# Attention, a dense block and routed experts on one core: where the first expert's hidden rows leave PSUM, when the small group's rows are scaled, and a rank computation cut in two

## The chip, the cores and the metric

The kernel runs on one core of a Trainium2 chip. The time is device microseconds (us) of one execution; a kernel's time is the median of its runs. The kernel before was run three times: 752.45 us median, 751.44 to 753.85.

## What is computed

Three blocks in a row, in float32. Attention over 4 batches, 12 heads, 448 positions and 64 channels with a tanh cap on the scores; a dense block with a SoLU and a layer norm on the 1792 tokens that come out; and a mixture of 8 experts, in which every token goes to one expert:

```python
logits = x @ w_gate + modality_bias[modality_id]
e_idx = np.argmax(logits, axis=1)
...
for e in range(E):
    mask = e_idx == e
    h = np.maximum(x[mask] @ w1[e], 0.0)
    out[mask] = gate_w[mask, None] * (h @ w2[e])
```

Which tokens go to which expert is known only when the dense block has produced the logits of the last token tile.

## The kernel before

The 1792 tokens are 14 tiles of 128. Each float32 operand of a large product is split into a high part and a remainder (names ending in `h` and `l`; ScalarE, ACT, casts the high part, VectorE, DVE, subtracts it), and TensorE (PE) makes three products of them: high by high, high by low, low by high. Products collect in PSUM; ACT and DVE empty it.

The program runs in four stretches. Up to some 430 us, attention and most of the dense block are interleaved on PE. Then come the last token tiles of the dense block with the **routing** between them. Then the **first expert**, the one that most of the first ten tiles chose, with 256 tokens, which starts before the routing is complete. Then the **slots** of a fixed list, `D` (512 tokens), `H` (128), `D`, `F` (256), `H`, with two **small groups** `T` of 32 tokens served beside the two `D` slots. In these last stretches the order on every engine is the order in which the code is written: PE and DVE are held to it in the routing stretch, and all engines from the end of the first expert's first layer on.

The names that matter for the change:

- **Routing** (`route_group`, a generator that the driver steps with `next`). It runs for tiles 0 to 9, then for 10 to 12 (`ra`), then for 13 (`rb`). Its first stage (L256 to L266) makes one-hot rows `r_oh` of each token's expert from the logits `lg` (L654, read from the PSUM tile `y`) and their running count `cum`; the second (L273 to L306) makes each token's rank among its expert's tokens and from it the matrices `r_A` and `r_B`; the third multiplies these on PE into the list of tokens `r_pt` (L316). For tile 13 the counts of all experts follow (`route_counts`, L366 to L379), `route_sums` on PE, `r_cmp` (L395), and at the end the index tables by which GpSimd (POOL) gathers the slots' rows.
- **First expert.** `e_weights` loads a block of its weights into `e_raw` (three buffers, L1031, queue of SyncE, SP), and splits it on ACT (L1033) and DVE (L1034) into `winh`/`winl` (first layer) and `wouh`/`woul` (second). The driver interleaves these steps with the rest (`next(ew)`). `e_h` makes the first layer (L1048 to L1052): 6 blocks of depth `d` by 8 blocks `f` of 128 hidden channels by 3 products of 256 columns. It collects in two PSUM tiles `e_ph` of two banks each, blocks 0 to 3 in the first and 4 to 7 in the second. In the last depth block, after every second `f`, ACT writes `e_hh` (L1055) and DVE `e_hl` (L1056) from the two blocks that are complete. `e_o` makes the second layer (L1068 to L1070): 8 blocks `f` by two token tiles (`e_po`, two more PSUM tiles) by 6 products. PSUM tiles of this size come from a ring of three, so the second `e_po` lies where the first `e_ph` was.
- **Between the blocks of `e_o`** stands the preparation of the first slot (`lead`, `first`, in `run_slots`): before blocks 3 to 6 the transposes of D's four token tiles (`s_tr`, L1221 to L1225), each emptied by ACT and DVE and followed by a weight split `wh_D`, `wl_D` (L1190, L1191); before block 7 the small group: DVE scales its 32 gathered rows `ygT` (`t_sc`, L1340 to L1342) and PE transposes them (`t_tr`, L1349) into `tpT`. After `e_o` PE goes on with D's first layer (`s_h`, L1247 to L1249, PSUM `phD`).

Of the kernel before, what the change touches and what calls it, by code (L numbers as in the profile page):

```python
# [14 lines left out]
AF = mybir.ActivationFunctionType  # L15
ALU = mybir.AluOpType
# [9 lines left out]
ND = DM // P  # L26
# [60 lines left out]
def attn_moe_kernel(ctx, tc, qt, kt, vv, cap, w_in, w_out, g_ln, ids, w_gate, mbias, w1, w2, out):  # L87
# [164 lines left out]
    def route_group(K, tp, psR, atile, a, b):  # L252
        n = b - a
        oh = K["oh"][:, a:b, :]
        kk = tp.tile([P, n, NE], F32, name=f"kk{a}")
        dve.tensor_tensor(kk, lg[:, a:b, :], nmx[:, a:b].unsqueeze(2).to_broadcast([P, n, NE]), op=ALU.add)  # L256
        dve.scalar_tensor_tensor(kk, kk, 0.0, K["rev"][:, a:b, :], op0=ALU.is_equal, op1=ALU.mult)
        fm = tp.tile([P, n], F32, name=f"fm{a}")
        dve.tensor_reduce(fm, kk, axis=AX.X, op=ALU.max)
        dve.tensor_tensor(oh, kk, fm.unsqueeze(2).to_broadcast([P, n, NE]), op=ALU.is_equal)  # L260
        pr = atile(f"pr{a}")[:, 0, :n * NE].rearrange("p (t e) -> p t e", e=NE)
        prev = rstate.get("cum")
        last = b == NTILE
        cum = tp.tile([P, NE], F16, name=f"cum{a}")
        if n == 1:
            dve.tensor_tensor(cum, prev, oh[:, 0, :], op=ALU.add)  # L266
        yield
        mm = []
        if prev is not None:
            mm.append((pr, K["ones"], prev.unsqueeze(1).to_broadcast([P, n, NE])))  # L270
        for t in range(n - 1):
            mm.append((pr[:, t + 1:, :], K["ones"], oh[:, t:t + 1, :].to_broadcast([P, n - 1 - t, NE])))
        pe.matmul(pr, K["tri"], oh, start=True, stop=not mm)  # L273
        for i, (o, l, r) in enumerate(mm):
            pe.matmul(o, l, r, start=False, stop=(i == len(mm) - 1))
        if n > 1:
            cs = tp.tile([P, NE], F32, name=f"cs{a}")
            dve.tensor_reduce(cs, oh.rearrange("p t e -> p e t"), axis=AX.X, op=ALU.add)
            if prev is None:
                dve.tensor_copy(cum, cs)  # L280
            else:
                dve.tensor_tensor(cum, cs, prev, op=ALU.add)
        rstate["cum"] = cum
        if last:
            route_total(K)
        pm = tp.tile([P, n, NE], F32, name=f"pm{a}")
        dve.tensor_tensor(pm, pr, oh, op=ALU.mult)
        if last:
            yield
            r1 = route_counts(K, tp)  # L290
            yield
            route_sums(K, r1)
        rf = tp.tile([P, n], F32, name=f"rf{a}")
        dve.tensor_reduce(rf, pm, axis=AX.X, op=ALU.add)
        ri, pl, ph = (tp.tile([P, n], I32, name=f"{x}{a}") for x in ("ri", "pl", "ph"))
        dve.tensor_copy(ri, rf)
        dve.tensor_scalar(pl, ri, P - 1, None, op0=ALU.bitwise_and)
        dve.tensor_scalar(ph, ri, 7, None, op0=ALU.logical_shift_right)
        A, Bm = K["A"][:, a:b, :], K["B"][:, a:b]
        dve.tensor_tensor(A, K["io128"].unsqueeze(1).to_broadcast([P, n, P]),  # L300
                          pl.unsqueeze(2).to_broadcast([P, n, P]), op=ALU.is_equal)
        rm = tp.tile([P, n, NR], F16, name=f"rm{a}")
        dve.tensor_tensor(rm, K["io14"].unsqueeze(1).to_broadcast([P, n, NR]),
                          ph.unsqueeze(2).to_broadcast([P, n, NR]), op=ALU.is_equal)
        dve.tensor_tensor(rm, rm, K["tid"][:, a:b].unsqueeze(2).to_broadcast([P, n, NR]), op=ALU.mult)
        dve.tensor_tensor(Bm, oh.unsqueeze(3).to_broadcast([P, n, NE, NR]),  # L306
                          rm.unsqueeze(2).to_broadcast([P, n, NE, NR]), op=ALU.mult)
        if last:
            cmp_ = route_expert(K, tp)
        yield  # L310
        if last:
            pe.matmul(rstate["sm"][:1, 16:16 + NS], K["ones"][:NE, 0:1], cmp_.rearrange("p a b -> p (a b)"), start=True, stop=True)
        if a == 0:
            rstate["pt"] = psR.tile([NE * NR, P], F32, name="r_pt")
        for t in range(a, b):
            pe.matmul(rstate["pt"], K["B"][:, t].rearrange("p a b -> p (a b)"), K["A"][:, t, :],  # L316
                      start=(t == 0), stop=(t == b - 1), skip_group_check=True)
        if a == 0:
            route_early(K, tp, psR)
        if last:  # L320
            yield from route_end(K, tp)
# [673 lines left out]
    ee = {}  # L995
# [41 lines left out]
    def e_h():  # L1037
        xh, xl = ee["xh"], ee["xl"]
        ph = []
        hh, hl = ([mp.tile([P, 4, SLOT], F32R, tag="m4", name=f"e_{x}{q}", bufs=4) for q in range(2)] for x in ("hh", "hl"))  # L1040
        ee["hh"], ee["hl"] = hh, hl
        for d in range(ND):
            for f in range(NF):
                if d == 0 and f % 4 == 0:
                    ph.append(atile(f"e_ph{f // 4}").rearrange("p a (b c) -> p (a b) c", c=SLOT))
                o = ph[f // 4][:, f % 4, :]
                c = slice(f * P, (f + 1) * P)
                pe.matmul(o, winh[d][:, c], xh[:, d, :], start=(d == 0 and f % 2 == 0), stop=False, skip_group_check=True)  # L1048
                yield
                pe.matmul(o, winh[d][:, c], xl[:, d, :], start=False, stop=False, skip_group_check=True)  # L1050
                yield
                pe.matmul(o, winl[d][:, c], xh[:, d, :], start=False, stop=(d == ND - 1), skip_group_check=True)  # L1052
                if d == ND - 1 and f % 2:
                    q, r = f // 4, slice(f % 4 - 1, f % 4 + 1)
                    act.activation(hh[q][:, r, :], ph[q][:, r, :], AF.Relu)  # L1055
                    dve.scalar_tensor_tensor(hl[q][:, r, :], ph[q][:, r, :], 0.0, hh[q][:, r, :], op0=ALU.max, op1=ALU.subtract)  # L1056
                yield
    def e_o(step):
        po = [atile(f"e_po{i}") for i in range(2)]
        for f in range(NF):  # L1060
            step(f)
            for i in range(2):
                o = slice(i * P, (i + 1) * P)
                hh, hl = ee["hh"][f // 4][:, f % 4, o], ee["hl"][f // 4][:, f % 4, o]
                for hf in range(2):
                    c = slice(hf * HD, (hf + 1) * HD)
                    p = po[i][:, hf, :HD]
                    pe.matmul(p, hh, wouh[f][:, c], start=(f == 0), stop=False)  # L1068
                    pe.matmul(p, hh, woul[f][:, c], start=False, stop=False)
                    pe.matmul(p, hl, wouh[f][:, c], start=False, stop=(f == NF - 1))  # L1070
        for i in range(2):
            ob = g2.tile([P, DM], F32, tag="tm", name=f"e_ob{i}", bufs=NTM)
            act.activation(ob[:, :HD], po[i][:, 0, :HD], AF.Copy, scale=ga0[:, i:i + 1])
            dve.tensor_scalar(ob[:, HD:], po[i][:, 1, :HD], ga0[:, i:i + 1], None, op0=ALU.mult)
            pool.indirect_dma_start(out=oview("E", i), out_offset=IndirectOffsetOnAxis(ap=sidx0[:, i:i + 1], axis=0),
                                    in_=ob, in_offset=None, bounds_check=NT, oob_is_err=False)
# [18 lines left out]
    def run(k):  # L1095
        for _ in range(k):
            msteps.pop(0)[1]()
# [9 lines left out]
    with tc.manual_schedule(engines={ET.PE, ET.DVE}):  # L1107
        run(4)
        ra, rb = (route_group(K, rt, psR, atile, *x) for x in groups)
        ew = weights()  # L1110
        next(ra)
        next(ew)
        run(5)
        next(ra)
        run(3)
        next(rb)
        next(ew)
        run(3)
        next(ra, None)
        run(3)  # L1120
        next(rb)
        next(rb)
        next(ew)
        run(4)
        eh = e_h()
        for steps, subs in EHS:
            run_h(steps)
            next(rb, None)
            for _ in range(subs):
                next(ew)  # L1130
    hand = ExitStack()
    hand.enter_context(tc.manual_schedule())
    for _ in eh:
        pass
    for _ in ew:
        pass
    for pl_ in (rt, xp, wi, psR):
# [253 lines left out]
    def run_slots(seq, small, lead=None):  # L1391
# [48 lines left out]
        def first(i):  # L1440
            if i < len(cols(seq[0])):
                s_tr(seq[0], (i,))
            elif smalls:
                t_sc(smalls[0])
                t_tr(smalls[0])
                if smalls[1:]:
                    t_gather(smalls[1])
# [160 lines left out]
```

## Time and profile before

| | |
|---|---|
| median of 3 runs | 752.45 us (751.44 to 753.85) |
| the profiled execution's own time | 751.36 us |
| its span, first to last instruction | 749.6 us |
| PE busy | 724.3 us, 97% of the span |
| DVE, ACT, POOL busy | 59%, 52%, 16% |
| mean granted clock of PE | 0.994 of full speed |
| idle of PE from 430 us to the end, longest parts | 2.8, 1.6, 1.1 and 0.5 us |

Times are read from the start of the span. A timeline row is: start, duration, engine, line, operation, output and inputs, shapes, how many, and in brackets the idle time of the engine before it with what ended that. PE's matmuls overlap: the duration of one is longer than the step from one to the next, and what a stretch costs is counted in steps. PEld is PE's weight load, SPq the queue from which SP issues transfers.

### The profile page before, as it was taken

Reading aid. Unit: us, or ns where it says so; the run is one execution under the profiler, and the core shown is the slowest. Engines: PE = TensorE matmul, PEld = TensorE weight load, DVE = VectorE, ACT = ScalarE, POOL = GpSimd, SP = SyncE. Lnnn points to the kernel's source line nnn. Section 1 sums busy time; section 2 is a strip of 40 time slices with the busy share of each in tenths; the row PEclk is TensorE's granted clock in tenths of the full one; section 3 lists DMA queues with packets and bytes.
Section 4 is the critical chain, followed back from the end, with each engine's and each line's share of the span. In section 5 each row is a group of like instructions: output and inputs, shape, how many; then the busy total and the mean of one; then the engine's idle time right before and its main releaser. Section 6 shows DMA issues by size and latency. Waiting matters only on the chain. (4 is left out here: it accounts for less than half of the span.)

```text
span 749.6 us, 11324 instructions
## 1 busy us (share of the span) xinstructions
PE 724.3 (97%) x4302; PEld 557.8 (74%) x4302; DVE 438.6 (59%) x782; ACT 387.1 (52%) x535; POOL 116.7 (16%) x214
## 2 busy tenths in 40 slices
PE   6999999999999999999999999989999999999994
PEld 2443556667767777677788999988879998799983
DVE  7999656747666567555367447746156173663621
ACT  5999756774575654666521224244154162643530
POOL 4221101111031021120031211303010220002010
PEclk9999999999999999999999999999999999999998
DMA  9776211211121110110003103559918369484520
GB/s 300 250 237 198 62 53 47 63 60 51 45 83 38 58 59 13 60 34 13 21 23 127 44 22 106 184 207 318 406 57 275 113 204 407 180 276 170 201 96 23
DMA packets 33426, 97.14 MB, mean 130 GB/s; under 512 B 4903, under 2 KB 11057, under 8 KB 33362
## 3 DMA queue, kind: packets, MB, share of 16 engines
q1 hardware_dynamic: 26546, 66.88, 26.4%
q0 software_dynamic: 6528, 29.42, 11.0%
q8 instruction: 35, 0.57, 0.3%
q14 instruction: 29, 0.24, 0.1%
q10 hardware_dynamic: 288, 0.03, 0.0%
HBM read 85.24 MB, written 11.27 MB: 129 GB/s over the span
## 5 line engine op out<-in xcount | busy, mean ns | idle before, releaser
L735 ACT ACTIVATE e<-sc,sc 112x896 f32<-112x896 f32 x96 | 94.5, 1005 | 66.7 <-PE sc L728 66.7
L740 ACT ACTIVATE e<-e,cap_t 112x896 f32<-112x896 f32 x96 | 98.1, 1045 | 1.7
L770 PE MATMUL av<-e,v 112*64 112x448 f32 x384 | 82.8, 552 | 0.0
L650 PE MATMUL y<-wouh,lh 128*128 128x392 f32 (+1 forms) x224 | 77.9, 348 | 0.5 <-DVE lg L654 0.5
L652 PE MATMUL y<-wouh,ll 128*128 128x392 f32 (+1 forms) x224 | 75.8, 338 | 0.1
L651 PE MATMUL y<-woul,lh 128*128 128x392 f32 (+1 forms) x224 | 75.9, 339 | 0.0
L595 PE MATMUL h<-winh,xh 128*128 128x512 f32 x168 | 68.9, 410 | 0.0
L597 PE MATMUL h<-winh,xl 128*128 128x512 f32 x168 | 66.0, 393 | 1.1 <-DVE xl L583 1.1
L596 PE MATMUL h<-winl,xh 128*128 128x512 f32 x168 | 65.6, 390 | 0.0
L770 PEld LDWEIGHTS av<-e,v 112*64 112x64 f32 x384 | 23.3, 136 | 35.4 <-issue 33.4
L650 PEld LDWEIGHTS y<-wouh,lh 128*128 128x128 f32 x224 | 42.0, 188 | 9.1 <-issue 7.1
L1191 DVE TENSOR_TENSOR wl_D<-raw_D,wh_D 128x768 fp32r<-128x768 f32 (+1 forms) x28 | 29.8, 1071 | 26.9 <-ACT wh_D L1190 26.6
L1191 DVE TENSOR_TENSOR wl_H<-raw_H,wh_H 128x768 fp32r<-128x768 f32 (+1 forms) x28 | 29.2, 1069 | 25.6 <-ACT wh_H L1190 25.6
L595 PEld LDWEIGHTS h<-winh,xh 128*128 128x128 f32 x168 | 31.6, 188 | 16.4 <-issue 9.3
L1320 PE MATMUL poD<-wh_D,hhD 128*128 128x384 f32 x128 | 43.0, 336 | 0.0
L1321 PE MATMUL poD<-wl_D,hhD 128*128 128x384 f32 x128 | 42.8, 334 | 0.0
L1322 PE MATMUL poD<-wh_D,hlD 128*128 128x384 f32 x128 | 42.8, 334 | 0.0
L652 PEld LDWEIGHTS y<-wouh,ll 128*128 128x128 f32 x224 | 42.1, 188 | 0.8 <-DVE ll L640 0.8
L651 PEld LDWEIGHTS y<-woul,lh 128*128 128x128 f32 x224 | 42.1, 188 | 0.6
L1190 ACT CAST wh_D<-raw_D 128x768 fp32r<-128x768 f32 (+1 forms) x28 | 26.1, 932 | 27.3 <-DMA raw_D<-in_w_dram 27.0
L1190 ACT CAST wh_H<-raw_H 128x768 fp32r<-128x768 f32 (+1 forms) x28 | 25.3, 941 | 25.5 <-PE phD L1248 7.6
L597 PEld LDWEIGHTS h<-winh,xl 128*128 128x128 f32 x168 | 31.5, 188 | 8.8 <-DVE xl L583 2.0
(373 smaller groups left out, 1605.8 us busy)
## 6 DMA issues: line engine op xcount, KB each, us to landing
rawc<-in_w_out_dram POOLq DMA_DIRECT2D x16, 384.0 KB, 4.3
rawc<-in_w_in_dram POOLq DMA_DIRECT2D x12, 512.0 KB, 4.3
raw_D<-in_w_dram SPq DMA_DIRECT2D x12, 512.0 KB, 5.7
wr_T<-in_w_dram SPq DMA_DIRECT2D x16, 384.0 KB, 6.9
raw_D<-in_w_dram SPq DMA_DIRECT2D x16, 384.0 KB, 4.3
wr_T<-in_w_dram SPq DMA_DIRECT2D x12, 512.0 KB, 9.8
raw_H<-in_w_dram SPq DMA_DIRECT2D x12, 512.0 KB, 6.6
raw_H<-in_w_dram SPq DMA_DIRECT2D x16, 384.0 KB, 3.7
```

The source lines that it names most:

```text
L595: pe.matmul(o, s["xh"][d], winh[d][:, c], start=(d == 0), stop=False)
L596: pe.matmul(o, s["xh"][d], winl[d][:, c], start=False, stop=False)
L597: pe.matmul(o, s["xl"][d], winh[d][:, c], start=False, stop=(d == ND - 1))
L650: pe.matmul(o, s["lh"][f], wouh[f][:, c], start=(f == 0), stop=False)
L651: pe.matmul(o, s["lh"][f], woul[f][:, c], start=False, stop=False)
L652: pe.matmul(o, s["ll"][f], wouh[f][:, c], start=False, stop=(f == NF - 1))
L735: act.activation(e, t[:CK, :, :S], AF.Tanh, scale=sc8[:CK])
L740: act.activation(e, e, AF.Exp, scale=cap_t[:CK])
L770: pe.matmul(o[64 * j:64 * j + 64, :S], v[:, c, 64 * j:64 * j + 64], et[b, p, c][:, j, :], start=(c == 0), stop=(c == 3))
L1190: act.copy(h_, raw)
L1191: dve.tensor_sub(l_, raw, h_)
L1320: pe.matmul(p, hh[:, f, o], wh[:, c], start=(f == 0), stop=False)
```

## The change

Three edits.

1. In `e_h` the emptying of the first `e_ph` tile stands after block 3, for the whole tile; that of the second stands after the end of `e_h`, behind two more weight steps. Each is done as before in two halves of 512 columns, ACT and then DVE.
2. The scaling of the small group's rows stands behind the first of D's four transposes, in place of just before its own.
3. In `route_group` a stop is added after `pm` for all but the last tile, so that for tiles 10 to 12 the second stage comes in two pieces, and the driver puts the first stage of tile 13 between them, makes the `r_pt` products three steps later, and one weight split (`winl_132`, depth block 3) after tile 13's counts.

```diff
@@ route_group
             r1 = route_counts(K, tp)
             yield
             route_sums(K, r1)
+        else:
+            yield
@@ e_h
-                if d == ND - 1 and f % 2:
-                    q, r = f // 4, slice(f % 4 - 1, f % 4 + 1)
-                    act.activation(hh[q][:, r, :], ph[q][:, r, :], AF.Relu)
-                    dve.scalar_tensor_tensor(hl[q][:, r, :], ph[q][:, r, :], 0.0, hh[q][:, r, :], op0=ALU.max, op1=ALU.subtract)
+                if d == ND - 1 and f == 3:
+                    e_relu(ph, 0)
                 yield
+        ee["ph"] = ph
+
+    def e_relu(ph, q):
+        hh, hl = ee["hh"][q], ee["hl"][q]
+        for i in range(2):
+            r = slice(2 * i, 2 * i + 2)
+            act.activation(hh[:, r, :], ph[q][:, r, :], AF.Relu)
+            dve.scalar_tensor_tensor(hl[:, r, :], ph[q][:, r, :], 0.0, hh[:, r, :], op0=ALU.max, op1=ALU.subtract)
@@ the driver
         run(3)
         next(rb)
-        next(ew)
-        run(3)
+        next(ra)
+        run(6)
         next(ra, None)
-        run(3)
         next(rb)
         next(rb)
+        next(ew)
         next(ew)
         run(4)
@@
     for _ in eh:
         pass
+    next(ew)
+    next(ew)
+    e_relu(ee["ph"], 1)
     for _ in ew:
         pass
@@ first, in run_slots
             if i < len(cols(seq[0])):
                 s_tr(seq[0], (i,))
+                if i == 0 and smalls:
+                    t_sc(smalls[0])
             elif smalls:
-                t_sc(smalls[0])
                 t_tr(smalls[0])
```

How the order of instructions moves, at three places. The number behind a name is that of the buffer; the changed kernel's line numbers are 2 to 12 higher.

**DVE in the routing stretch, before.** `r_B` is the last step of the second stage for tiles 10 to 12, `lg` to `cum_4272` belong to tile 13, `e_xl` is the low part of the first expert's rows.

```order
L306 TENSOR_TENSOR r_B<-r_oh,rm_4250 128x336
L654 SCALAR_TENSOR_TENSOR lg<-y_4216,sm_4106,bias_t 128x8
L656 TENSOR_REDUCE nmx<-lg 128x1
L256 TENSOR_TENSOR kk_4265<-lg,nmx 128x8
L257 SCALAR_TENSOR_TENSOR kk_4265<-kk_4265,r_rev 128x8
L259 TENSOR_REDUCE fm_4268<-kk_4265 128x1
L260 TENSOR_TENSOR r_oh<-kk_4265,fm_4268 128x8
L266 TENSOR_TENSOR cum_4272<-cum_4211,r_oh 128x8
L1034 TENSOR_TENSOR winl_132<-e_raw_3_4274,winh_126 128x1024
L1016 TENSOR_TENSOR e_xl<-e_xt_4280,e_xh 128x6x128
```

The same engine in the changed kernel, from the piece `pm` of tiles 10 to 12 on:

```order
L287 TENSOR_TENSOR pm_4239<-pr_4210,r_oh 128x24
L656 SCALAR_TENSOR_TENSOR lg<-y_4216,sm_4106,bias_t 128x8
L658 TENSOR_REDUCE nmx<-lg 128x1
L256 TENSOR_TENSOR kk_4252<-lg,nmx 128x8
L257 SCALAR_TENSOR_TENSOR kk_4252<-kk_4252,r_rev 128x8
L259 TENSOR_REDUCE fm_4255<-kk_4252 128x1
L260 TENSOR_TENSOR r_oh<-kk_4252,fm_4255 128x8
L266 TENSOR_TENSOR cum_4259<-cum_4211,r_oh 128x8
L296 TENSOR_REDUCE rf_4261<-pm_4239 128x3
```

and further on, behind tile 13's counts, of which the last two rows stand here:

```order
L380 TENSOR_SCALAR r_wn<-r_dv 8x1
L381 COPY r_wn<-r_wn 8x1
L1036 TENSOR_TENSOR winl_132<-e_raw_3_4334,winh_126 128x1024
L1036 TENSOR_TENSOR winl_133<-e_raw_4_4338,winh_127 128x1024
L296 TENSOR_REDUCE rf_4374<-pm_4318 128x1
```

Tile 13's seven steps, from `lg` to `cum`, moved ahead of the eight from `rf` to `r_B`; `winl_132` moved from ahead of `e_xl` to behind the counts `r_wn`, and stands ahead of the rank of tile 13 (`rf_4374`), at whose end `r_cmp` is.

**ACT at the end of the first expert's first layer, before** (the queue behind the cast of block 3 of `wouh`):

```order
L1033 CAST wouh_138<-e_raw_3_4471 128x768
L1055 ACTIVATE e_hh_4356<-e_ph_4360 128x512 x2
L1055 ACTIVATE e_hh_4357<-e_ph_4397 128x512 x2
L1033 CAST wouh_139<-e_raw_4_4588 128x768
L1033 CAST wouh_140<-e_raw_5_4592 128x768
L1033 CAST wouh_141<-e_raw_6_4596 128x768
L1033 CAST wouh_142<-e_raw_7_4600 128x768
```

and in the changed kernel:

```order
L1035 CAST wouh_138<-e_raw_3_4471 128x768
L1064 ACTIVATE e_hh_4356<-e_ph_4360 128x512 x2
L1035 CAST wouh_139<-e_raw_4_4584 128x768
L1035 CAST wouh_140<-e_raw_5_4588 128x768
L1064 ACTIVATE e_hh_4357<-e_ph_4397 128x512 x2
L1035 CAST wouh_141<-e_raw_6_4596 128x768
L1035 CAST wouh_142<-e_raw_7_4600 128x768
```

Two casts, whose rows wait for transfers, moved between the two PSUM tiles. DVE's queue moved in the same way.

**PE at the start of the second layer, before**, with the semaphores that a row waits for:

```order
L1068 MATMUL e_po_4659<-wouh_135,e_hh_4356 128x384 [waits Activation_49]
L1069 MATMUL e_po_4659<-woul_143,e_hh_4356 128x384
L1070 MATMUL e_po_4659<-wouh_135,e_hl_4358 128x384
L1068 MATMUL e_po_4659<-wouh_135,e_hh_4356 128x384
L1069 MATMUL e_po_4659<-woul_143,e_hh_4356 128x384
L1070 MATMUL e_po_4659<-wouh_135,e_hl_4358 128x384
L1068 MATMUL e_po_4660<-wouh_135,e_hh_4356 128x384 [waits PE_49]
```

and in the changed kernel:

```order
L1077 MATMUL e_po_4659<-wouh_135,e_hh_4356 128x384 [waits Activation_49]
L1078 MATMUL e_po_4659<-woul_143,e_hh_4356 128x384 [waits DVE_49]
L1079 MATMUL e_po_4659<-wouh_135,e_hl_4358 128x384 [waits DVE_49]
L1077 MATMUL e_po_4659<-wouh_135,e_hh_4356 128x384
L1078 MATMUL e_po_4659<-woul_143,e_hh_4356 128x384
L1079 MATMUL e_po_4659<-wouh_135,e_hl_4358 128x384
L1077 MATMUL e_po_4660<-wouh_135,e_hh_4356 128x384 [waits DVE_49,PE_49]
```

The first product into the second `e_po` tile, the last row, waits for DVE as well now: that is the release of the first `e_ph` tile, whose place it takes. In `e_h` the waits for DVE in the last depth block are gone.

**DVE beside D's transposes, before**, from the fourth token tile on:

```order
L1223 TENSOR_TENSOR xl_D_4698<-xtD_3_0_4790,xh_D_4697 128x3x128
L1223 TENSOR_TENSOR xl_D_4698<-xtD_3_1_4796,xh_D_4697 128x3x128
L1225 TENSOR_SCALAR gaD_4620<-ygD_3_4633 128x1
L1227 RECIPROCAL gaD_4620<-gaD_4620 128x4
L1191 TENSOR_TENSOR wl_D_3_4805<-raw_D_3_4657,wh_D_3_4804 128x1024
L1340 TENSOR_SCALAR gtT_4641<-ygT_4637 32x1
L1341 RECIPROCAL gtT_4641<-gtT_4641 32x1
L1342 TENSOR_SCALAR ygT_4637<-ygT_4637,gtT_4641 32x768
L1191 TENSOR_TENSOR wl_D_4_4838<-raw_D_4_4741,wh_D_4_4837 128x1024
```

and in the changed kernel, from the first token tile on:

```order
L1235 TENSOR_TENSOR xl_D_4698<-xtD_0_0_4699,xh_D_4697 128x3x128
L1235 TENSOR_TENSOR xl_D_4698<-xtD_0_1_4705,xh_D_4697 128x3x128
L1237 TENSOR_SCALAR gaD_4620<-ygD_0_4621 128x1
L1352 TENSOR_SCALAR gtT_4641<-ygT_4637 32x1
L1353 RECIPROCAL gtT_4641<-gtT_4641 32x1
L1354 TENSOR_SCALAR ygT_4637<-ygT_4637,gtT_4641 32x768
L1203 TENSOR_TENSOR wl_D_0_4716<-raw_D_0_4651,wh_D_0_4715 128x1024
L1235 TENSOR_TENSOR xl_D_4698<-xtD_1_0_4731,xh_D_4697 128x3x128
```

The three steps on `ygT` moved from behind `wl_D_3` to between the first token tile's `gaD` and `wl_D_0`, three tiles ahead.

## Rows read from the trace of the kernel before

**Rows 1.** Page, part 1: busy time of each engine, share, instructions.

```profile
PE 724.3 (97%) x4302; PEld 557.8 (74%) x4302; DVE 438.6 (59%) x782; ACT 387.1 (52%) x535; POOL 116.7 (16%) x214
```

**Rows 2.** PE's waits, 430 to 750: engine, line, releaser: total, times, longest.

```profile
PE e_ph L1048 <- DVE e_hl L1056: 2.8, 2, 1.4
PE tpT L1349 <- issue: 1.6, 1, 1.6
...
PE y L650 <- DVE lg L654: 0.5, 1, 0.5
```

**Rows 3.** Timeline of PE, end of the first expert's first layer.

```profile
488.84 0.28 PE L1052 MATMUL e_ph<-e_xh,winl 128*128 128x256 f32 x1
...
490.53 0.39 PE L1048 MATMUL e_ph<-e_xh,winh 128*128 128x256 f32 x1 [1.41 <-DVE e_hl L1056]
490.75 0.28 PE L1050 MATMUL e_ph<-e_xl,winh 128*128 128x256 f32 x1
...
491.94 0.28 PE L1052 MATMUL e_ph<-e_xh,winl 128*128 128x256 f32 x1
...
494.44 0.34 PE L1068 MATMUL e_po<-wouh,e_hh 128*128 128x384 f32 x1
...
500.71 0.82 PE L1221 MATMUL xtD<-ident,ygD 128*128 128x128 f32 x6
```

**Rows 4.** Timeline of ACT and DVE: the dense block's tile `lt`, second half.

```profile
461.04 0.59 ACT L639 CAST lh<-lt 128x512 fp32r<-128x512 f32 x1 [0.76 <-DVE ll L640]
...
461.66 0.69 DVE L640 TENSOR_TENSOR ll<-lt,lh 128x512 fp32r<-128x512 f32 x1 [0.65 <-ACT lh L639]
```

**Rows 5.** Timeline of DVE and PE, routing of tiles 10 to 13.

```profile
465.09 0.18 DVE L294 TENSOR_REDUCE rf<-pm 128x3 f32<-128x24 f32 x1
465.22 0.34 PE L652 MATMUL y<-wouh,ll 128*128 128x392 f32 x1
...
467.08 0.22 DVE L654 SCALAR_TENSOR_TENSOR lg<-y,sm,bias_t 128x8 f32<-128x8 f32 x1
...
468.41 1.22 DVE L1034 TENSOR_TENSOR winl<-e_raw,winh 128x1024 fp32r<-128x1024 f32 x1
469.55 0.95 DVE L1016 TENSOR_TENSOR e_xl<-e_xt,e_xh 128x768 fp32r<-128x768 f32 x1
...
475.33 0.17 DVE L395 TENSOR_TENSOR r_cmp<-r_io,r_sm 8x32 f16<-8x32 f32 x1
...
476.47 0.17 PE L312 MATMUL r_sm<-r_cmp,r_ones 8*1 8x32 f16 x1
```

**Rows 6.** Timeline: last blocks of `e_o`; below, the second small group's transposes.

```profile
511.64 0.34 PE L1070 MATMUL e_po<-wouh,e_hl 128*128 128x384 f32 x1
512.91 0.61 DVE L1342 TENSOR_SCALAR ygT<-ygT,gtT 32x768 f32<-32x768 f32 x1
513.62 0.53 PE L1349 MATMUL tpT<-ident,ygT 32*128 32x32 f32 x6 [1.65 <-issue]
...
517.63 0.60 PE L1247 MATMUL phD<-xh_D,wh_D 128*128 128x512 f32 x1
...
607.93 0.55 PE L1349 MATMUL tpT<-ident,ygT 32*128 32x32 f32 x6
608.41 0.45 PE L1320 MATMUL poH<-wh_H,hhH 128*128 128x384 f32 x1
```

**Rows 7.** By stretch, PE: us, busy (count), granted clock, DMA share, GB/s.

```profile
515.00:516.00 1.00, 1.00 (x4) 0.50 1.05 421
```

**Rows 8.** By stretch: PE, PEld, DVE, ACT, POOL busy, clock, DMA share, GB/s.

```profile
518.00:545.00 27.00, 27.00 (x120) 22.33 (x119) 6.81 (x7) 5.79 (x7) 6.32 (x6) 1.00 1.01 392
```

**Rows 9.** Timeline: last load of the small group's first-layer weights; their first use.

```profile
535.56 0.33 SPq L1185 DMA_DIRECT2D wr_T<-in_w_dram  x1
...
550.58 2.32 PEld L1360 LDWEIGHTS thT<-wr_T,txT 128*32 128x32 f32 x48 [0.35 <-issue]
```

**Rows 10.** Page, part 6: these loads: count, KB each, us to landing.

```profile
wr_T<-in_w_dram SPq DMA_DIRECT2D x12, 512.0 KB, 9.8
```

## The prediction

> **What bounds the kernel now.** I read the page's busy times first: PE is busy for 97% of the span, the next engine for 59% [rows 1]. So an edit can gain time only where PE stands still or runs slow, and whatever shortens such a place shortens the whole, as long as the stretches behind it find their data. The second view is therefore the table of PE's own waits in the second half of the program [rows 2]. The three edits lie on its entries: two waits of 1.4 us for DVE inside `e_h`, one of 1.6 us before the small group's transposes `tpT`, one of 0.5 us for the logits of the last token tile. Third come the timelines of these places, because the idle view understates them: it counts from the end of the last product, while a product ends some two steps after the next could have begun. Fourth is the granted clock, which stands at 0.50 (1.2 of 2.4 GHz) right behind the `tpT` wait [rows 7] and at 1.00 before and after.
>
> **Edit 1, the first expert's hidden rows.** Before, products stop twice in the last depth block: the third pair's first product follows the last one of block 1 only when `e_hl` has read the PSUM tile. From 488.84 to 490.75 two steps pass in 1.91 us. A step is (491.94 - 490.75) / 10 = 0.119 us, so the stop costs 1.91 - 0.24 = 1.67 us, and the second of the two the same: 3.35 us [rows 3]. The change removes both.
>
> It adds a wait elsewhere. Let T be the end of block 3's last product. Blocks 4 to 7 (12 steps of 0.119) and the first six products of `e_o` (steps of (500.71 - 494.44) / 36 = 0.174 [rows 3]) bring PE to the first product into the second `e_po` tile at T - 0.16 + 1.43 + 1.04 = T + 2.3. That tile lies where the first `e_ph` was, and so waits for all of its emptying: now four instructions (ACT, DVE, ACT, DVE) that start at T. No row shows the four of `e_ph` in a row. The nearest is the same pattern in the dense block: there the second ACT waits 0.76 us for the first DVE, then takes 0.59, and DVE 0.69 [rows 4]; with the first ACT's 0.59 the chain is 2.7 us. So the new wait is about 0.4, with 0.1 for restarting. If ACT did not wait for DVE the chain would be 0.59 + 0.59 + 2 x 0.69 less what overlaps, some 2.05 us, and there is no wait; if the first product with `e_hl` (T + 1.6) waited for both halves, it would cost 1.1. I take 0.5, since the pattern of [rows 4] is the same code with other names: edit 1 gives **2.85**, between 2.2 and 3.35.
>
> The Trainium skill (PSUM — Partial Sum Buffer, Specifications) says that ScalarE and VectorE may use PSUM at the same time at full rate while they are in different banks, and the two halves are in different banks. By that sentence the chain is the short one and the sum below is 0.5 better. The row says otherwise for this program: the second ACT there does wait, whatever the banks allow.
>
> The second tile's emptying now stands behind two casts and splits on ACT and DVE. It is needed at block 4 of `e_o`, 4 x 12 steps and one set of transposes (some 9 us) after `e_o` starts; two casts, two splits and the chain are some 5 us. It costs nothing; without that cover it would cost the chain, 2.7.
>
> **Edit 2, the small group's rows.** Before, the last product of block 6 starts at 511.64; the transposes could follow one step later, at 511.8, but the scaling of `ygT`, behind D's transposes and splits on DVE, ends at 513.52, and they start at 513.62 [rows 6]. Then the clock is at half [rows 7], and D's first product starts only at 517.63. Without the wait the transposes take 0.48 to the next product, as the second small group's do (607.93 to 608.41 [rows 6]), and block 7's 12 products 0.28 + 11 x 0.174 = 2.2: D's first product at 514.5. That is 3.05 us earlier, and the 0.60 us of that product itself, at half clock, shrink by 0.2: **3.2 us**, 1.7 of stall and 1.5 of clock. If the clock falls all the same the 1.7 remain; the upper end is 3.3. On DVE the three steps (0.61 for the last [rows 6], the two on one column about 0.18 each like `rf` [rows 5], 1.0 in all) now stand three transposes earlier, ahead of `wl_D_0`. PE's next block of `e_o`, 12 steps or 2.1 us, hides them; the next transposes but one need DVE's copies of the first PSUM tiles, so uncovered they would cost at most their 1.0, once. I price them at nothing.
>
> **Edit 3, the rank.** The logits' wait: `lg` of tile 13 reads a product that ends at 465.22 + 0.34 = 465.6, yet runs at 467.08, behind the 2.0 us from `rf` to `r_B` [rows 5]. In the new order it runs at 465.6, and the 0.5 of idle goes, some 0.75 in steps. What it costs: tile 13's seven steps take 468.41 - 467.08 = 1.33, so they end at 466.95, `r_B` at 468.94, and `e_xl` starts there in place of 469.55 [rows 5]: 0.61 earlier, with the counts. But `winl_132` (469.55 - 468.41 = 1.14 [rows 5]) now stands behind the counts, ahead of tile 13's rank, so `r_cmp` comes 1.14 - 0.61 = 0.53 later: it ends at 475.5 + 0.53 = 476.03. PE, 0.75 early, asks for it at 475.7 in place of 476.47 [rows 5], and waits until 476.1. Of the 0.75 there remains **0.35**, between 0 and 0.75. The transfer that reuses `winl_132`'s raw buffer starts some 4 us later (469.6 before, 473.4 now, by the sums above); it brings the first block of `wouh`, wanted when `e_o` starts, at 490.7 after edit 1: nothing, and if that cover were gone, up to those 4 us.
>
> **The sum.** 2.85 + 3.2 + 0.35 = 6.4 us. None of the waits in that table lies between 518 and 733, and from 518 to 545 PE is busy 27.00 of 27.00 us [rows 8], so the shift reaches the end. Against the profiled execution's own 751.36 us: 745.0. That execution is 1.1 below the median (752.45) and at the lower end of the three; what the other runs lost there isn't shown, and part of it may lie in the waits that go. I put the forecast at **745.3 us**, a third of the 1.1 above the sum. About 0.3% (2.3 us) is what a measurement of this kernel can tell from no change.
>
> **Rivals.**
> *The clock falls elsewhere.* Half a clock followed the 1.65 us stall but not the two of 1.4, and the new waits of 0.4 in `e_o` and the routing lie close to what went. One such fall costs the 1.5 us above: 746.5 against the sum. For it: the row of 0.50 [rows 7] shows how little suffices. Against: what remains is far shorter than what was removed. The Trainium skill (TensorE: Matmul & The Clock Gate, What's actually happening) says that what the gate looks at runs freely, so that the same kernel changes clock at other places from run to run. By that rule the 1.5 is in some runs and not in others; no run here shows it twice. 12%.
> *The hand-off moves in full.* `e_hl` is wanted whole by its first reader and the rank gains nothing: 2.2 + 3.2 + 0 = 5.4, 746.0. Against it: the first reader takes 128 columns of the first half, and the release of the PSUM tile is listed as a wait of its own. 12%.
> *Not what it says.* The transposes wait all the same (for `ygT` or for their PSUM tile, of which there are two), and the clock falls with them: edit 2 gives nothing, edits 1 and 3 at their lower ends 2.2: 749.2, inside what can't be told from no change against 751.4. For it: the wait is filed under "issue", with no releaser. Against: DVE's row ends 0.1 before the transposes start. 4%.
> *Slower: PE outruns the loads.* From 518 to 545 the DMA engines are full (1.01, 392 GB/s [rows 8]). Their stream starts behind the first expert's last weight loads, and moves with edits 1 and 3 alone, by my estimate the 3.7 us that PE gains up to the end of `e_h` (3.35 + 0.35), while PE comes 6.4 earlier: 2.7 us of slack go. The place is the small group's first layer: its last weight load is issued at 535.56 [rows 9] and lands 9.8 later [rows 10], 545.4, wanted from 550.58 [rows 9]: slack 5.2. It decides only from a delay of 5.2 - 2.7 = 2.5 us more, and to end 2.3 us slower than before the loads must be late by 2.5 + 6.4 + 2.3 = 11.2 us: 751.4 + 2.3 = 753.7. 2%.
>
> **How the numbers follow.** Forecast 70%, rivals 12, 12, 4 and 2%. Low end: the upper ends 0.75 + 3.35 + 3.3 = 7.4 give 744.0; 0.7 below that for the spread of runs, 743.3. High end: the lower ends 0 + 2.2 + 1.7 = 3.9 give 747.5 against the profiled run, and most of the 1.1 to the median on top: 748.3. Faster by over 0.3%: forecast and the first two rivals, 94%, less 2 for a median that takes back more: 0.92. Within 0.3%: 0.05. Slower: 0.03.
>
> **What would show it.** In the profile after: no wait of `e_ph` for DVE; one wait of 0.3 to 0.6 us at the seventh product of `e_o`; `tpT` one step behind its predecessor and the granted clock at 1.00 until D's first product; `lg` of tile 13 around 465.6, no wait of PE for it, and one of about 0.4 for `r_cmp`; D's first product at 517.63 - 6.2 = 511.4. The prediction is wrong if that product is at 511.4 and the end isn't 6.4 earlier (then the loads came late), if the clock falls at another place, or if `e_o` waits for more than 1 us at its start.

## The result and the profile after

The changed kernel takes 745.25 us (median of 4 runs, 744.78 to 746.22) against 752.62 us before (4 runs, 751.44 to 753.85): a ratio of 0.9905, 95% interval 0.9892 to 0.9918. The forecast was 745.3 us. The profiled execution after took 745.61 us with a span of 743.9 us, against 751.36 and 749.6.

Page, part 1, after:

```profile
PE 722.9 (97%) x4302; PEld 556.0 (75%) x4302; DVE 439.5 (59%) x782; ACT 387.1 (52%) x535; POOL 115.8 (16%) x214
```

The count of instructions on each engine is the same [rows 1]. Of the 5.7 us by which the span is shorter, PE's busy time accounts for 1.4 (724.3 less 722.9) and its idle time for the other 4.3. PE's waits from 430 us to the end, after (columns as in [rows 2]):

```profile
PE poH L1334 <- PEq L1573: 0.9, 1, 0.9
PE e_po L1077 <- DVE e_hl L1065: 0.4, 1, 0.4
PE pr L273 <- DVE ga L1019: 0.3, 1, 0.3
```

The three entries on which the edits lay [rows 2] are gone. The wait at `poH` stood there before too (1.1 us). Two short ones are new. One, of 0.4 us at `e_po`, was forecast; the other, of 0.3 us at `pr`, was not.

Timeline of PE, ACT and DVE after, where [rows 3], [rows 5] and [rows 6] show it before:

```profile
466.09 0.34 PE L654 MATMUL y<-wouh,ll 128*128 128x392 f32 x1
466.54 0.23 DVE L656 SCALAR_TENSOR_TENSOR lg<-y,sm,bias_t 128x8 f32<-128x8 f32 x1 [0.61 <-PE y L654]
...
469.85 0.95 DVE L1018 TENSOR_TENSOR e_xl<-e_xt,e_xh 128x768 fp32r<-128x768 f32 x1
...
470.85 0.17 PE L273 MATMUL pr<-r_oh,r_tri 128*128 128x8 f16 x1 [0.33 <-DVE ga L1019]
...
476.77 0.17 DVE L397 TENSOR_TENSOR r_cmp<-r_io,r_sm 8x32 f16<-8x32 f32 x1
...
476.99 0.17 PE L314 MATMUL r_sm<-r_cmp,r_ones 8*1 8x32 f16 x1
...
490.30 0.60 ACT L1064 ACTIVATE e_hh<-e_ph 128x512 fp32r<-128x512 f32 x1 [6.20 <-PE e_ph L1054]
...
491.50 0.34 PE L1077 MATMUL e_po<-wouh,e_hh 128*128 128x384 f32 x1
491.65 0.60 ACT L1064 ACTIVATE e_hh<-e_ph 128x512 fp32r<-128x512 f32 x1 [0.76 <-DVE e_hl L1065]
...
492.28 0.69 DVE L1065 SCALAR_TENSOR_TENSOR e_hl<-e_ph,e_hh 128x512 fp32r<-128x512 f32 x1 [0.66 <-ACT e_hh L1064]
492.38 0.34 PE L1079 MATMUL e_po<-wouh,e_hl 128*128 128x384 f32 x1
493.12 0.41 PE L1077 MATMUL e_po<-wouh,e_hh 128*128 128x384 f32 x1 [0.41 <-DVE e_hl L1065]
...
500.89 0.61 DVE L1354 TENSOR_SCALAR ygT<-ygT,gtT 32x768 f32<-32x768 f32 x1
...
509.25 0.34 PE L1079 MATMUL e_po<-wouh,e_hl 128*128 128x384 f32 x1
509.52 0.56 PE L1361 MATMUL tpT<-ident,ygT 32*128 32x32 f32 x6
```

D's first product starts at 512.20. `ygT` is ready 8.0 us before it is wanted, and `tpT` follows its predecessor by 0.27 us, where 1.98 us passed before [rows 6]. The granted clock behind it (by stretch, columns as in [rows 8]) is at 1.00, where it was 0.50 [rows 7]:

```profile
508.00:512.00 4.00, 4.00 (x26) 3.71 (x26) 2.78 (x6) 2.83 (x5) 0.92 (x1) 1.00 1.00 357
512.00:513.00 1.00, 1.00 (x7) 0.87 (x6) 1.00 (x2) 0.60 (x2) 0.00 (x0) 1.00 1.00 378
513.00:515.00 2.00, 2.00 (x11) 1.62 (x10) 1.74 (x3) 0.91 (x1) 1.25 (x2) 1.00 1.08 404
515.00:518.00 3.00, 3.00 (x15) 2.49 (x14) 1.13 (x2) 0.83 (x1) 2.39 (x3) 1.00 0.95 314
518.00:545.00 27.00, 27.00 (x124) 22.09 (x124) 8.16 (x10) 7.75 (x11) 2.74 (x3) 1.00 0.86 347
```

**One table for all executions.** Each row is one profiled execution. The start of the stretch differs by up to 3 us from execution to execution, so what the edits do is read from differences of start times on PE: from the last product with the logits (466.09 above) to the first product of `e_h` (472.74), to the product of `r_cmp` (476.99), to the first of `e_o` (491.50), to `tpT` (509.52), to D's first product (512.20). The last column but one is what is left of the span behind D's first product; the last is the usual step from one product of `e_h` to the next. All in us; the kernels from the third row on are those of the experiments.

| execution | to `e_h` | to `r_cmp` | to `e_o` | to `tpT` | to D | sum | rest | `e_h` product |
|---|---|---|---|---|---|---|---|---|
| before | 7.22 | 4.03 | 17.97 | 19.18 | 4.01 | **52.41** | 231.97 | 0.119 |
| after | 6.65 | 4.25 | 14.51 | 18.02 | 2.68 | **46.11** | 231.70 | 0.117 |
| hidden_only | 7.21 | 4.06 | 14.62 | 19.73 | 4.07 | **49.69** | 232.08 | 0.119 |
| scale_only | 7.25 | 4.03 | 18.01 | 17.37 | 2.72 | **49.38** | 231.83 | 0.119 |
| rank_only | 6.68 | 4.21 | 17.98 | 19.10 | 4.10 | **52.07** | 232.37 | 0.119 |
| no_scale | 6.65 | 4.24 | 14.63 | 19.73 | 4.22 | **49.47** | 231.97 | 0.119 |
| scale_fourth | 6.65 | 4.25 | 14.63 | 18.45 | 2.68 | **46.66** | 232.29 | 0.119 |
| second_tile_later | 6.66 | 4.24 | 14.52 | 17.43 | 2.69 | **45.54** | 231.85 | 0.117 |
| rank_reordered | 6.25 | 3.99 | 14.04 | 18.07 | 2.72 | **45.07** | 231.64 | 0.113 |
| all_three | 6.25 | 3.99 | 14.04 | 17.43 | 2.69 | **44.40** | 231.83 | 0.113 |
| changed_again | 6.68 | 4.21 | 14.65 | 18.02 | 2.68 | **46.24** | 231.96 | 0.119 |
| shifted | 6.65 | 4.25 | 14.56 | 18.00 | 2.68 | **46.14** | 231.85 | 0.118 |
| reordered_shifted | 6.26 | 4.05 | 14.58 | 18.03 | 2.71 | **45.63** | 231.68 | 0.118 |
| same_place | 6.65 | 4.24 | 14.55 | 18.01 | 2.72 | **46.17** | 232.05 | 0.118 |

### The profile page after: what moved, and what is told of

Read it like the earlier page. It is cut to its first block, busy times and chain, and to the rows that moved or that the text cites. A ratio compares the mean times of both kernels' runs of the same rounds, so it can differ in the third digit from the quotient of the medians.

```text
span 743.9 us, 11323 instructions
## 1 busy us (share of the span) xinstructions
PE 722.9 (97%) x4302; PEld 556.0 (75%) x4302; DVE 439.5 (59%) x782; ACT 387.1 (52%) x535; POOL 115.8 (16%) x214
## 5 line engine op out<-in xcount | busy, mean ns | idle before, releaser
L772 PE MATMUL av<-e,v 112*64 112x448 f32 x384 | 84.3, 560 | 0.0
L1260 PE MATMUL phD<-xl_D,wh_D 128*128 128x512 f32 x96 | 37.4, 389 | 0.0
```

The source lines that it names most:

```text
L772: pe.matmul(o[64 * j:64 * j + 64, :S], v[:, c, 64 * j:64 * j + 64], et[b, p, c][:, j, :], start=(c == 0), stop=(c == 3))
```

## The experiments

**The edits one by one.** Three kernels make one edit each on the kernel before, one takes the second edit out of the changed kernel. They were timed together, beside 23 runs of the kernel before (752.67 us).

First edit alone:

```diff
-                if d == ND - 1 and f % 2:
...
+                if d == ND - 1 and f == 3:
+                    e_relu(ph, 0)
...
+    next(ew)
+    next(ew)
+    e_relu(ee["ph"], 1)
```

> The kernel before with the first edit alone (the first expert's hidden rows emptied by whole PSUM tile). Theory: 2.85 us faster than before (3.35 less 0.5), 749.8 against 752.6; PE has no wait in e_h, one of about 0.4 us at the seventh product of e_o, and the small group's transposes still stand some 1.65 us behind the scaling of ygT, with the clock at 0.50 behind them, only some 3 us earlier in the program. Rival: the scaling of ygT on DVE hangs on the loads of D's weights, not on PE; then what e_h gives back is lost again in front of the small group's transposes, whose wait grows from 1.65 to about 4.5 us, and the time is that of before (752.6, less 0.3 at most).

Measured: 749.26 us (12 runs), ratio 0.9958 (0.9943 to 0.9973). The stretch to `e_o` is 17.97 - 14.62 = 3.35 us shorter, the next one 0.55 longer; the sum is 2.72 us less. The wait at `tpT` has not grown, so the rival falls: DVE's work ahead of `ygT` comes earlier when PE does.

```profile
PE tpT L1359 <- issue: 1.7, 1, 1.7
```

Second edit alone:

```diff
+                if i == 0 and smalls:
+                    t_sc(smalls[0])
             elif smalls:
-                t_sc(smalls[0])
```

> The kernel before with the second edit alone (ygT scaled beside D's first column). Theory: 3.2 us faster than before, 749.4 against 752.6: no wait at the small group's transposes, clock 1.00 until D's first product, the two stops of e_h unchanged at 1.4 us each. Rival, the clock falls there for another reason than the wait: 1.7 us faster, 750.9, with a stretch at 0.50 around D's first product all the same.

Measured: 749.08 us (6 runs), ratio 0.9955 (0.9938 to 0.9972). Of the 3.03 us by which the sum is shorter, 1.81 lie ahead of `tpT` and 1.29 behind it. The two stops of 1.4 us in `e_h` are unchanged.

Third edit alone:

```diff
+        else:
+            yield
...
         next(rb)
-        next(ew)
-        run(3)
+        next(ra)
+        run(6)
         next(ra, None)
-        run(3)
         next(rb)
         next(rb)
+        next(ew)
         next(ew)
```

> The kernel before with the third edit alone (rank part of the last tiles in two stages). Theory: 0.35 us faster by the trace, 752.3 against 752.6, too little for the times; in the trace no wait for the logits of the last token tile, a wait of 0.3 us of pr for e_xl, which holds its PSUM buffer, and a gap of 0.4 us ahead of r_cmp's product. Rival, pr's wait is a matter of that one execution: it is gone here, and the gain is 0.6 us.

Measured: 751.93 us (12 runs), ratio 0.9993 (0.9982 to 1.0004), which the times can't tell from no change. The sum of the stretches is 0.34 us shorter: 0.54 gained ahead of `e_h`, 0.18 lost ahead of `r_cmp`. The wait of `pr` is there again:

```profile
PE pr L273 <- DVE ga L1019: 0.3, 1, 0.3
```

The changed kernel without its second edit:

```diff
                 s_tr(seq[0], (i,))
-                if i == 0 and smalls:
-                    t_sc(smalls[0])
             elif smalls:
+                t_sc(smalls[0])
                 t_tr(smalls[0])
```

> The changed kernel with the second edit taken back (first and third stay). Theory: 3.2 us slower than the changed kernel, 748.4, or 4.2 us faster than before by the medians (745.25 + 3.2 = 748.45): the wait at the small group's transposes is back with about 1.7 us, and the clock stands at 0.50 for some 3 us behind it. Rival, the clock fell in the kernel before for another reason: only the wait comes back, 747.0, with the clock at 1.00. Rival, the scaling hangs on D's weights: the wait is about 4.5 us, and the time 751 or more.

Measured: 749.37 us (6 runs), ratio 0.9953 (0.9934 to 0.9971); the sum is 3.36 us above that of the changed kernel (1.71 ahead of `tpT`, 1.54 behind it, 0.12 in `e_h`). The time is 1.0 us above the expected 748.4, which lies inside the interval (747.7 to 750.5 by the 752.67 beside it); the rival of 747.0 doesn't, and the clock decides against it too. Wait and half clock are back together, as these rows of PE's waits, and below them of the stretches, show:

```profile
PE tpT L1361 <- issue: 1.7, 1, 1.7
```

```profile
512.00:513.00 1.00, 0.69 (x7) 0.68 (x8) 0.21 (x1) 0.13 (x1) 0.00 (x0) 0.90 0.94 356
513.00:514.00 1.00, 1.00 (x4) 1.00 (x5) 0.00 (x0) 1.00 (x2) 0.89 (x1) 0.50 1.02 402
514.00:515.00 1.00, 1.00 (x5) 1.00 (x4) 0.83 (x1) 0.14 (x1) 0.03 (x1) 0.50 1.03 412
515.00:516.00 1.00, 1.00 (x5) 1.00 (x4) 0.69 (x2) 0.58 (x1) 0.00 (x0) 0.50 1.01 406
```

The parts add up: 2.72 + 3.03 + 0.34 = 6.09 us by the stretches, against 6.30 for the whole change (6.17 in its second execution, changed_again), and 0.9958 x 0.9955 x 0.9993 = 0.9906 by the times, against 0.9905.

**Does any stop here bring the clock down?**

```diff
-                if i == 0 and smalls:
+                if i == 3 and smalls:
                     t_sc(smalls[0])
```

> The changed kernel with the scaling of ygT beside D's fourth column and not its first, ahead of the split of weights that follows. Theory, the clock falls behind a stop of PE of about 1.65 us and not behind a short one: the transposes come about 0.55 us late (509.95 against 509.42 in the profile of the changed kernel), the clock stays at 1.00, and D's first product comes 0.5 to 0.6 us later than in the changed kernel. Rival, any stop at this place, under full DMA load, brings the clock down: a stretch at 0.50 behind it, and D's first product 2 us later.

Measured: by the sum D's first product comes 0.55 us later, 0.43 of it ahead of `tpT` and 0.12 in the products of `e_h`; from `tpT` to D it is 2.68 us, as in the changed kernel. PE's wait and the stretch behind it:

```profile
PE tpT L1361 <- issue: 0.4, 1, 0.4
```

```profile
511.00:513.00 2.00, 2.00 (x12) 1.88 (x11) 1.51 (x2) 1.52 (x4) 0.47 (x1) 1.00 1.00 383
```

The DMA engines are full here (1.00), and the clock stays at 1.00, so the rival falls, by one execution. The stop of 0.4 us costs itself; at the same place the one of 1.7 us costs nearly twice itself (1.71 + 1.54).

**What the new wait at the second `e_po` is for.**

```diff
-        for f in range(NF):
-            step(f)
-            for i in range(2):
+        for f, i in ((0, 0), (1, 0), (0, 1), (1, 1), *((f, i) for f in range(2, NF) for i in range(2))):
...
```

> The changed kernel, with the first two hidden blocks of e_o taken for the first token tile and only then for the second, so that the first product into the second e_po stands at place 13 and not 7. Theory, that product waits for the PSUM buffer of the first e_ph, whose four emptying instructions end 2.7 us after its last product: six products of 0.174 us cover the 0.4 us, the wait is gone, and from the first product of e_o to the one at place 13 there pass 12 steps, 2.1 us (2.7 in the changed kernel). Rival, it waits for the data of the second half of e_hh or e_hl, or for anything that stands in PE's order and not at this tile: the wait stays at 0.4 us or moves to place 7.

Measured: no wait of `e_po` is left, and the stretch from `e_o` to `tpT` falls from 18.02 to 17.43 us. The thirteenth product starts 2.08 us behind the first:

```profile
493.73 0.34 PE L1080 MATMUL e_po<-wouh,e_hh 128*128 128x384 f32 x1
...
495.81 0.34 PE L1080 MATMUL e_po<-wouh,e_hh 128*128 128x384 f32 x1
```

The product that had waited takes the same operands as before, only later. That alone would not tell a wait for the buffer from one for its data. But its data were there: in the changed kernel the first six products of `e_o`, for which no wait is listed, read the same `wouh`, and from the same ACT instruction the same half of `e_hh`. So what it waited for is its PSUM buffer. The chain that frees the buffer is as long as before: DVE's second half starts at 494.51 here and takes 0.69, so it ends at 495.20, 0.6 us before the buffer is written.

**The rank part.** One more step of the weights (the number 2 in `EHS`) stands behind `r_cmp` and not ahead of it.

```diff
-EHS = ((8, 1), (16, 1), (18, 3))
+EHS = ((8, 2), (16, 1), (18, 3))
...
+            if i == 0:
+                next(ee["mid"])
...
-        next(ra)
+        ee["mid"] = ra
         run(6)
-        next(ra, None)
         next(rb)
         next(rb)
         next(ew)
-        next(ew)
-        run(4)
+        run(1)
+        next(ra, None)
+        run(3)
```

> The changed kernel with the first e_xl ahead of the rank steps of tiles 10 to 12 on DVE, their product r_pt three products later on PE, and one split of weights moved from ahead of r_cmp to behind it. Theory: the wait of pr (0.33 us) goes, since the buffer that it takes is emptied 1 us earlier, and r_cmp, 1.2 us earlier on DVE, is there before PE asks: the gap ahead of its product falls from 0.41 to 0.12 us. Together 0.6 us, by the stretch from the last product with the logits to the first e_h product behind r_cmp. Rival, DVE is full here and the work that is pushed back stops PE next: r_pt waits for r_B, or the first product of e_h for the second e_xl, or route_sums for r_wn, with 0.3 us or more.

Measured: the waits of `pr` and ahead of `r_cmp`'s product are gone, 6.25 + 3.99 against 6.65 + 4.25: 0.66 us. DVE has room for what was pushed back; no new wait appears in PE's list. The step ahead of `r_cmp`'s product stays at 0.21 us (476.72 to 476.93) although `r_cmp` ends at 476.51, so the 0.12 expected there was too little, and in the changed kernel only 0.2 of its 0.41 us were a wait. Unforeseen: the stretch through `e_h` is 0.47 us shorter too. Its products come every 0.113 us in place of 0.117 to 0.119, from the first block to the last, with the clock at 1.00 in both.

**Both reorderings together**, beside the changed kernel:

> The changed kernel with both reorderings: the second token tile's first products later, and the rank steps as in rank_reordered. Theory, the gains add, since each lies in another place: against the changed kernel 0.57 us at the second e_po, 0.66 us up to r_cmp's product, and 0.47 us in e_h, if its products run at 0.113 us again instead of 0.117; from the last product with the logits to D's first product 44.4 us (46.1 in the changed kernel), and the time 1.7 us below that of the changed kernel beside it. Rival, the faster products were a matter of that one execution: 44.9 us and 1.2 us.

> The changed kernel once more, beside the version with both reorderings. Theory: 745.3 us, 46.1 us from the last product with the logits to D's first product, products of e_h at 0.117 to 0.119 us, while the start (the wait for the first load, 6.3 to 7.6 us in the runs so far) moves the whole by a microsecond from one execution to the next.

Measured: the version with both takes 744.71 us (5 runs), ratio 0.9897 (0.9874 to 0.9921); the changed kernel beside it 747.91 us (6 runs, 745.35 to 748.65), ratio 0.9933 (0.9911 to 0.9955). The two intervals overlap, so the times alone don't separate them; the stretches do, 44.40 us, as forecast, against 46.24. The products of `e_h` run at 0.113 us again, so the rival falls.

The times expected were missed. The changed kernel was to take 745.3 us and took 2.6 more; the version with both was to be 1.7 us faster and was 3.2. The profiled executions show where this lies. That of the changed kernel took 748.31 us here and 745.61 in the result: 2.31 of these 2.70 us lie ahead of the last product with the logits (468.40 against 466.09), and the stretches from there to D differ by 0.13. Of the 3.2 us between the two versions, then, only the 1.84 of the stretches are shown to come from the reorderings.

From 430 us on one wait is left in the version with both:

```profile
PE poH L1339 <- PEq L1578: 1.0, 1, 1.0
```

**Why `e_h` runs faster there.** The buffers `e_xh` and `e_xl`, which every product of `e_h` reads, had moved by 224 bytes in that version. Three kernels move them and leave the order of the instructions, two that of the changed kernel and one that of rank_reordered; the first edit below is made on both.

```diff
-        xh = rt.tile([P, ND, SLOT], F32R, name="e_xh")
-        xl = rt.tile([P, ND, SLOT], F32R, name="e_xl")
+        xh, xl = (rt.tile([P, ND * SLOT + 16], F32R, name=f"e_x{x}")[:, 8:8 + ND * SLOT]
+                  .rearrange("p (d c) -> p d c", c=SLOT) for x in "hl")
```

> The changed kernel with e_xh and e_xl, the moving operands of e_h, each 32 bytes further inside a tile that is 64 bytes longer, so that their first byte falls on a multiple of 64 bytes in the partition, as it does in rank_reordered (143456 before, 143360 now, 143232 there); the order of the instructions stays. Theory, the place of the moving operand sets the pace of e_h: its products come every 0.113 us, as in rank_reordered, and e_h is 0.5 us shorter (14.0 us from r_cmp's product to the first of e_o). Rival, it was the order or the execution: 0.117 to 0.119 us as in the changed kernel.

> rank_reordered with e_xh and e_xl shifted by 32 bytes in the same way, here off the multiple of 64 bytes on which they stood. Theory of the place: the products of e_h come every 0.117 to 0.119 us again, and the 0.47 us that e_h had gained are gone (14.5 us from r_cmp's product to the first of e_o). Rival: they stay at 0.113 us.

```diff
-        xl = rt.tile([P, ND, SLOT], F32R, name="e_xl")
+        xl = rt.tile([P, ND * SLOT + 56], F32R, name="e_xl")[:, :ND * SLOT].rearrange("p (d c) -> p d c", c=SLOT)
```

> The changed kernel with a longer e_xl, so that e_xh and e_xl begin at byte 143232 and 149376 of the partition, exactly as in rank_reordered and in the version with both reorderings; the order of the instructions stays that of the changed kernel. Theory, the place alone sets the pace: the products of e_h come every 0.113 us, and from r_cmp's product to the first of e_o 14.0 us pass. Rival, the order of the work beside them has its part: 0.117 us or more, 14.5 us.

Measured, one execution each: 0.118 us in all three (same_place: 14.55 us through `e_h`). The shift took the fast pace away from the reordered kernel; the fast place did not bring it to the changed one. So the place of the operands alone isn't the cause, nor is the order alone, and the rule of 64 bytes falls. The two kernels at 0.113 have order and place in common, in one execution each; the changed kernel's own two executions differ by less (0.117 and 0.119). What makes the pace stays open.

## Why the prediction held

- **What bounds.** PE was the bound and stayed it: what PE lost in idle time [rows 2] and at half clock [rows 7] is what the kernel gained, and the rest behind D's first product is the same within the scatter (231.97 before, 231.70 after, 231.64 to 232.37 in all).
- **Edit 1**, forecast 2.85: 2.72 alone. Both terms are right, the two stops at 3.35 and the new wait at 0.5 (0.55 to 0.6). The working time of the chain behind it was taken from the same pattern in the dense block [rows 4], where ACT's second half waits 0.76 us for DVE's first; after, it waits 0.76 here too. The Trainium skill (PSUM — Partial Sum Buffer, Specifications) lets ACT and DVE read PSUM together in different banks. In this program they don't: in the rows above ACT's second half is released by the end of DVE's first (0.76 us, DVE `e_hl`), so the row of before was the right guide. With the short chain of that sentence there would be no wait at `e_po`, and the sum would have been 0.5 us too good.
- **Edit 2**, forecast 3.2, as 1.7 of stall and 1.5 of clock: 1.81 and 1.29 alone, 1.71 and 1.54 beside the other edits. Two small errors of the working offset each other. From 514.5 to 517.63 it is 3.13 us, where the working has 3.05; and `tpT` follows its predecessor by 0.27 us, where it has 0.16.
- **Edit 3**, forecast 0.35: 0.34, but by another way than its working. The gain at the logits is there in full: `lg` runs at 466.54 less the 0.87 us by which this execution is late, 465.67, where 465.6 was forecast, and no wait for it is left. Of it, 0.2 is lost sooner than forecast, at `pr`: it takes the PSUM buffer of the first `e_xt`, and so waits for DVE's first `e_xl`, now that PE is there earlier than DVE. In the trace of before `pr` already stands right behind it: `e_xl` ends at 470.50 [rows 5], and `pr` starts 0.05 us later, as it does after (470.80 and 470.85).

```profile
470.55 0.17 PE L273 MATMUL pr<-r_oh,r_tri 128*128 128x8 f16 x1
```

  At `r_cmp` only 0.2 us are then lost, in place of 0.4. The step that failed is "PE, 0.75 early, asks for it at 475.7": it left out the wait for that buffer, which stands in PE's order just ahead. The 0.35 holds all the same, and not by luck: `r_cmp` on DVE is what ends the stretch. It ends at 476.94 less 0.87, which is 476.07 where 476.03 was forecast, and what PE loses ahead of it is not lost again there.
- **The sum and the median.** 6.30 us by the stretches, which end where D's first product starts. There the forecast had 6.2, its 6.4 less the 0.2 of that product itself, which the scatter of the rest hides. The profiled execution after took 745.61, not 745.0: it lost 0.87 us before the routing (466.09 against 465.22), for the reason in the last section. D's first product, set at 511.4, came at 512.20, which is 511.33 without that loss. That the median (745.25) came within 0.1 us of the forecast is luck. The third of 1.1 us that the forecast put on top was a guess, and the same kernel's median beside all_three was 747.91, inside the stated range and 2.6 us higher.
- **The rivals.** No clock fall moved to another place behind the edits; the hand-off of `e_hl` cost what the tile's release costs and no more; `tpT` doesn't wait. The loads were never near: the last load of the small group's first-layer weights is issued at 530.33 and its first use is at 544.96, 14.6 us, where 15.0 lay between them before [rows 9]:

```profile
530.33 0.33 SPq L1197 DMA_DIRECT2D wr_T<-in_w_dram  x1
...
544.96 2.32 PEld L1372 LDWEIGHTS thT<-wr_T,txT 128*32 128x32 f32 x48 [0.35 <-issue]
```

  They moved with PE (530.33 less 0.87 is 6.1 us ahead of 535.56), where the estimate had let them move by 3.7 alone.

## What to carry to other kernels

An engine's stop must be priced by the steps between the instructions around it and by the clock behind it: the profile's list put 1.6 us on `tpT`, and removing it brought 3. When, as here, a whole tile's emptying is moved off the bound, the next wait is at the next user of its buffer; a few products of another tile put in between cover it. After making the bound engine earlier, look through everything that it meets next for buffers that another engine empties, not only for the data that it reads.

## What the runs showed that was not expected

**The clock falls at two places early in the program, in some executions only.** In the changed kernel's second profile (changed_again) PE stands still for 0.74 us at 23 us (the wait `pt`), and the clock is at 0.50 from 24 to 27 us; from 82 to 84 us it is at 0.50 again, with PE busy throughout. Below, the first product behind the wait, and stretches:

```profile
23.79 0.86 PE L545 MATMUL pt<-ident,to 128*128 128x128 f32 x3 [0.74 <-ACT e L737]
```

```profile
24.00:25.00 1.00, 1.00 (x5) 0.54 (x6) 0.97 (x3) 1.00 (x3) 0.00 (x0) 0.50 1.00 352
...
80.00:82.00 2.00, 2.00 (x15) 1.43 (x17) 1.13 (x4) 1.89 (x5) 0.00 (x0) 0.97 0.29 108
82.00:84.00 2.00, 2.00 (x10) 0.45 (x10) 1.90 (x5) 0.86 (x1) 0.00 (x0) 0.50 0.00 0
```

Of the 14 profiled executions, the one before and two others (scale_fourth, all_three) show neither fall; in these the last product with the logits starts at 465.2 to 465.7 us. Seven show the first alone, 466.1 to 467.4; one (rank_reordered) shows the second alone, 466.7; three show both, 467.8 to 468.4. These falls and the wait for the first load (PE's first product starts at 6.3 to 7.7 us) set when the routing starts. From PE's first product to the last with the logits 457.96 to 458.24 us pass without a fall, 459.61 to 459.95 with one, and 461.05 to 461.29 with both: a fall, with the wait of PE that stands ahead of the first one, costs 1.4 to 2.0 us. The 0.87 us lie here: the execution after has one fall, 1.79 us by this measure, and started 0.92 us earlier. The execution profiled before is one of the three without a fall, which fits its place 1.1 us below the median.

At the first place the fall goes with a stop of PE. In all ten executions that show it PE waits for ACT ahead of `pt`, from 22.3 to 23.9 us on and for 0.43 to 0.75 us, and the clock falls 0.7 to 1.8 us behind the beginning of that wait; the four others have no such wait there. No edit here takes the stop away by itself, so that it brings the fall isn't shown. At the second place PE is busy, and of the changed kernel's two executions one has the fall and one hasn't. The Trainium skill (TensorE: Matmul & The Clock Gate, What's actually happening) says that the point at which the clock changes differs between runs of the same kernel; the second place agrees with it. By that rule the fall behind `tpT` could have been absent in some executions too; in the four that have the stop there it never was.

**Behind the 1.7 us stop the fall was regular.** The clock fell behind `tpT` in all four kernels that have this stop, and in none of the ten executions without it. Two stops of 1.4 us in `e_h` left the clock at 1.00 in all three kernels that have them. A stop's length alone doesn't tell, then: 0.43 us at 23 us (scale_only) was followed by a fall, 1.4 us at 490 us and 0.4 us at `tpT` weren't.
